# Attention and a multiplicative feed-forward network: score matmuls on (64,32) array tiles, a new order of the opening loads, and the g vectors spread by a matmul

## The chip, the core and the metric

The kernel runs on one core of one Trainium2 chip. The metric is the device time of one execution in microseconds (us), the median of ten executions. In the profile, PE is the matrix engine and PEld its weight loads, DVE the vector engine, ACT the scalar engine, POOL the GpSimd engine, and SP an engine that here only issues DMAs. The engines run side by side, each works through its own instructions in order, and semaphores tie them together.

## The reference

Attention over 8 batches of 12 heads with 448 rows of 64 elements, where q and k are normalised (RMS norm) first; then a feed-forward network over the 3584 rows of 768:

```python
def _attn_ref(q, k, v, g_q, g_k):
    def rmsnorm(x, g):
        rms = np.sqrt(np.mean(x * x, axis=-1, keepdims=True) + 1e-06)
        return x / rms * g
    q_n, k_n = (rmsnorm(q, g_q), rmsnorm(k, g_k))
    scores = 1.0 / np.sqrt(q.shape[-1]) * np.matmul(q_n, k_n.transpose(0, 1, 3, 2))
    scores = scores - np.max(scores, axis=-1, keepdims=True)
    attn = np.exp(scores)
    attn = attn / (np.sum(attn, axis=-1, keepdims=True) + 1e-09)
    return np.matmul(attn, v).astype(np.float32)

def _moe_ref(x, w1, w2, w3, w_out):
    a = x @ w1
    b = x @ w2
    h = a * b @ w3
    return (h @ w_out).astype(np.float32)
```

q, k and v are (8, 12, 448, 64), w1 and w2 are (768, 1024), w3 is (1024, 1024), w_out is (1024, 768). All inputs and the output are float32.

## The kernel before

**Quads.** The attention is cut into 24 quads, each of four heads of one batch (three quads a batch). A row index of a head is split over 112 partitions and J = 4 column groups. For each quad the kernel loads q and k on SP's queue (`load_qk`, L98, three buffers each) and v on POOL's queue with a cast to bf16 (`load_v`, L116, four buffers); squares q and k on ACT (L157); sums them on DVE (L166); forms alpha = 1/rms on ACT as exp(-0.5 ln) (L176, L177); scales q by alpha (L188), by the product of both g vectors `g_b` (L195), and k by alpha (L201). The result `qks` is transposed to `qkT` (two heads stacked on 128 partitions): on PE for quads 0 to 4 (L220, copied out by DVE at L223), by a DMA transpose on SP's queue (L210) for the later ones.

**Slots.** The main loop goes over 25 x 4 slots, t = 4i + sl. A slot writes its work in this order: the scores and exp of a quarter of quad i (`qk_exp`, L226); up to one of the three products of quad i-1 (`pv_set`, L248: the row sums, then the two halves of P times v); up to four of the waiting weight loads (`wq`); filler work for PE; and last the preparation steps that the table `agenda` puts into this slot. Each engine executes in the order of this text, so that an instruction that waits holds up all that is written behind it on its engine.

**The scores.** One slot makes two `sc` tiles of 112 x 2 x 512 in PSUM (two buffers). Each comes from two matmuls at L235: 64 contraction rows (one head each, partitions 0 to 63 and 64 to 127), 112 output columns, 448 streamed columns. ACT takes exp of each tile (L244). The other large matmuls are in column tiles of 32: `pv` at L259 (112 x 32), and all of the feed-forward network in `narrow` (L312, L314: 128 x 32, four tiles side by side, one set for each 128-row block).

**The product of w3 and w_out.** The kernel makes w34 = w3 @ w_out once, in the opening slots: eight transposes of w3 (`w3_transpose`, L290, PE at L293, copied out by DVE at L288) and sixteen units (`w34_unit(fc, nh)`, L298, PE at L301, copied out by ACT at L286). nh is the half of w_out's columns that a unit uses. `W34_SLOTS` gives one or two of these 24 steps to each of slots 1 to 13; the list `w34q` orders them, with units of half 1 coming `LAG` steps behind those of half 0. From slot 15 on the fillers are the feed-forward network of the batches whose attention is done (`ffn1_a`, `ffn1_b`, `ffn2`); what is left of it runs after the last quad, from about 348 us.

**The opening.** POOL first loads both g vectors, each spread over 112 partitions by its DMA (L401, L402). DVE multiplies them at L424 and makes `g_b` at L425, written ahead of the first L188. q of quad 0 goes on SP's queue and k on ACT's, in two halves each; SP then issues q and k of quads 1 and 2 (the loads of quad 2 are written in slot 0). POOL then copies one column of the last head of k (L410, the tile `gate`), which holds POOL's queue until that half of k has landed. Behind it stand: the first half of w_out (two DMAs), w3 blocks 0 to 3, v of quad 0, the second half of w_out (two DMAs); and in the slots w3 blocks 4 and 5, v of quad 1, w3 blocks 6 and 7, v of quad 2, sixteen DMAs of w1 and w2, v of quad 3. POOL's loads share eight semaphores, so that each issue waits until the one eight places before it has landed. Sixteen warm-up matmuls (L395) keep PE busy meanwhile.

Of the kernel before, what the change touches and what calls it, by code (L numbers as in the profile page):

```python
# [8 lines left out]
FP = mybir.dt.float32  # L9
BF = mybir.dt.bfloat16  # L10
MULT = mybir.AluOpType.mult
# [7 lines left out]
def kernel(  # L19
# [13 lines left out]
    nc = tc.nc  # L33

    B, H, S, D = q.shape
    NP = 112
    J = S // NP
    HQ = 4
# [4 lines left out]
    CF = DFF // 128  # L43
# [4 lines left out]
    const = ctx.enter_context(tc.tile_pool(name="const", bufs=1))  # L48
# [12 lines left out]
    N_PE_T = 5  # L61
    N_SQ_ACT = 24
    W34_EV = "DA"
    LAG = 4
    SHIFT = [0, 0, 0, -1, -2, -3, -4]
    PREP_1 = {
        "sq0": -4, "red0": -4, "sq1": -4, "red1": -3, "alpha": -3,
# [11 lines left out]
    w_outs = const.tile([128, CF, DM], BF, name="w_outs")  # L79
    w3s = big_pool.tile([128, CF, DFF], BF, tag="big", name="w3s")  # L80
    w3T = big_pool.tile([128, CF, DFF], BF, tag="big", name="w3T")
    gq_b = const.tile([NP, D], FP, name="gq_b")
    gk_b = const.tile([NP, D], FP, name="gk_b")
    g_b = const.tile([NP, D], BF, name="g_b")
    ident = const.tile([128, 128], BF, name="ident")
    ones = const.tile([NP, HALF], BF, name="ones")
# [1 line left out]
    gate = const.tile([NP, 1], FP, name="gate")  # L88
# [9 lines left out]
    def load_qk(i, split=1, k_eng=None):  # L98
        b, m = divmod(i, NQB)
        s = st[i]  # L100
        s["q"] = load_pool.tile([NP, HQ, J, D], FP, tag="q", name="q_sb")
        s["k"] = load_pool.tile([NP, HQ, J, D], FP, tag="k", name="k_sb")
        n = HQ // split
        for h0 in range(0, HQ, n):
            for t_sb, src, eng in (
                (s["q"], q, nc.sync),
                (s["k"], k, k_eng or nc.sync),
            ):
                eng.dma_start(
                    out=t_sb[:, h0 : h0 + n].rearrange("p h j d -> p h (j d)"),  # L110
                    in_=src[b, HQ * m + h0 : HQ * m + h0 + n].rearrange(
                        "h (p j) d -> p h (j d)", j=J
                    ),
                )

    def load_v(i):  # L116
        b, m = divmod(i, NQB)
        s = st[i]
        s["v"] = load_pool.tile([NP, HQ, J, D], BF, tag="v", name="v_sb", bufs=4)
        nc.gpsimd.dma_start(  # L120
            out=s["v"].rearrange("p h j d -> p h (j d)"),
            in_=v[b, HQ * m : HQ * (m + 1)].rearrange("h (p j) d -> p h (j d)", j=J),
        )
# [9 lines left out]
    def load_w3(c):  # L133
        nc.gpsimd.dma_start(
            out=w3s[:, c, :],
            in_=moe_w3.rearrange("(c p) f -> p c f", p=128)[:, c, :],
        )

    def load_wout(nh, c):
        nc.gpsimd.dma_start(  # L140
            out=w_outs[:, 4 * c : 4 * c + 4, nh * NH : (nh + 1) * NH],
            in_=moe_w_out.rearrange("(c p) n -> p c n", p=128)[
                :, 4 * c : 4 * c + 4, nh * NH : (nh + 1) * NH
            ],
        )


    def prep_sq(i, pr, on_act=False):
# [77 lines left out]
    def qk_exp(i, g):  # L226
        s = st[i]
        if g == 0:
            s["P"] = att_pool.tile([NP, HQ, J, S], BF, tag="P", name="P")
        pr, t = divmod(g, 2)  # L230
        qkT, P = s["qkT"], s["P"]
        for jk in (2 * t, 2 * t + 1):
            sc = sc_psum.tile([NP, 2, 512], FP, tag="sc", name="sc")
            for u in range(2):
                nc.tensor.matmul(  # L235
                    out=sc[:, u, 0:S],
                    lhsT=qkT[u * D : (u + 1) * D, pr, J + jk, :],
                    rhs=qkT[u * D : (u + 1) * D, pr, 0:J, :].rearrange(
                        "d j p -> d (j p)"
                    ),  # L240
                    start=True,
                    stop=True,
                )
            nc.scalar.activation(  # L244
                out=P[:, 2 * pr : 2 * pr + 2, jk, :], in_=sc[:, :, 0:S], func=AF.Exp
            )
# [151 lines left out]

    with tc.manual_schedule():

        nc.gpsimd.dma_start(out=gq_b, in_=g_q.unsqueeze(0).broadcast_to([NP, D]))  # L401
        nc.gpsimd.dma_start(out=gk_b, in_=g_k.unsqueeze(0).broadcast_to([NP, D]))  # L402
        nc.vector.memset(warm_t, 0.0)
        nc.vector.memset(eps_t, 64e-6)
        nc.vector.memset(ones, 1.0)
        load_qk(0, split=2, k_eng=nc.scalar)
        nc.scalar.preload_act_table_set("natural_log_exp_and_others")
        load_qk(1)
        make_identity(nc, ident)
        nc.gpsimd.tensor_copy(out=gate, in_=st[0]["k"][:, HQ - 1, 0, 0:1])  # L410
        load_wout(0, 0)
        load_wout(0, 1)
        for c in range(4):
            load_w3(c)
        load_v(0)
        load_wout(1, 0)
        load_wout(1, 1)
        warm(16)
        for pr in range(2):
            prep_sq(0, pr, on_act=True)  # L420
            prep_red(0, pr)
            prep_alpha(0, 2 * pr, 2 * pr + 2)
            if pr == 0:
                nc.vector.tensor_tensor(out=gq_b, in0=gq_b, in1=gk_b, op=MULT)  # L424
                nc.vector.tensor_scalar(  # L425
                    out=g_b, in0=gq_b, scalar1=8.0, scalar2=None, op0=MULT
                )
            prep_scale(0, pr, pe=True)
            if pr == 0:
                prep_pe_transpose(0, 0)  # L430

        wq = [lambda c=c: load_w3(c) for c in range(4, CF)]
        wq.insert(2, lambda: load_v(1))
        wq.append(lambda: load_v(2))
        for h in range(HQ):
            for half in range(2):
                for w, src in ((w1s, moe_w1), (w2s, moe_w2)):
                    wq.append(
                        lambda w=w, src=src, h=h, half=half: load_w12(w, src, h, half)
                    )  # L440
        wq.append(lambda: load_v(3))

        w34q = [lambda: w3_transpose(0), lambda: w3_transpose(1)]
        for fc in range(CF + LAG):
            if fc < CF:
                w34q.append(lambda fc=fc: w34_unit(fc, 0))
            if fc + 2 < CF:
                w34q.append(lambda fc=fc: w3_transpose(fc + 2))
            if fc >= LAG:
                w34q.append(lambda fc=fc: w34_unit(fc - LAG, 1))  # L450

        def prep_part(n, part):
            pe = n < N_PE_T
            if part[:2] == "sq":
                prep_sq(n, int(part[2]), on_act=n < N_SQ_ACT)
            elif part[:3] == "red":
                prep_red(n, int(part[3]))
            elif part == "alpha":
                prep_alpha(n)
            elif part[:2] == "sc":  # L460
                prep_scale(n, int(part[2]), pe=pe)
            elif pe:
                prep_pe_transpose(n, int(part[1]))


        agenda = {}
        for n in range(1, NQ):
            shift = SHIFT[min(n, len(SHIFT)) - 1]
            table = PREP_1 if n == 1 else PREP
            for part, rel in table.items():  # L470
                agenda.setdefault(max(0, 4 * n + rel + shift), []).append((n, part))

        for i in range(NQ + 1):
            for sl in range(4):
                t = 4 * i + sl
                mine = agenda.pop(t, [])
                for n, part in mine:
                    if part == "load":
                        load_qk(n)
                if i < NQ:  # L480
                    qk_exp(i, sl)
                if t == 0:
                    prep_pe_transpose(0, 1)
                seen = len(fillers)
                if i > 0 and sl < 3:
                    pv_set(i - 1, sl)
                fresh = fillers[seen:]
                if sl == 0 and 4 <= i + 1 < NQ:
                    load_v(i + 1)
                for _ in range(4):  # L490
                    if wq:
                        wq.pop(0)()
                if t in W34_SLOTS:
                    for _ in range(W34_SLOTS[t]):
                        if w34q:
                            w34q.pop(0)()
                elif not w34q:
                    left = (14 - t) % 12 + 1
                    old = len(fillers) - sum(1 for f in fillers if f in fresh)
                    fill(min(2, -(-old // left)))  # L500
                for n, part in mine:
                    if part[0] == "t":
                        prep_part(n, part)
                for n, part in mine:
                    if part[0] != "t" and part != "load":
                        prep_part(n, part)
        fill(len(fillers))
# [28 lines left out]
```

## Time and profile before

| what | value |
|---|---|
| median of ten executions | 391.9 us (391.3 to 394.57) |
| the profiled execution's own time | 391.85 us |
| its span from the first to the last instruction | 390.0 us |
| the 16 warm-up matmuls L395 | end at 7.76 us |
| first scores (slot 0) start | 13.64 us |
| first transpose of w3 starts | 20.73 us |
| first feed-forward matmul starts | 68.83 us |
| last slot with scores (t = 95) | about 346 us |
| score matmuls L235 | 384, 57.4 us busy |
| exp L244 | 192 of 915 ns, 165.3 us busy |

The span begins with the first instruction and ends with the last; what lies around it is 1.85 us in this execution. "Busy" is the time in which at least one instruction of the group was under way: four matmuls side by side count once.

### The profile page before, as it was taken

What the parts mean: (1) busy time and instruction counts of PE and PEld (TensorE: products, weight loads), DVE (VectorE), ACT (ScalarE), POOL (GpSimd) and SP (SyncE); (2) the same over time, 40 slices, a digit from 0 to 9 for tenths busy, and PEclk for the clock granted to TensorE, in tenths of its full rate; (3) what the DMA queues carried; (4) which work ended last, traced back from release to release, by engine and by line L of the source; (5) the groups of instructions that cost most, each with busy time, mean ns of one, the idle gap of its engine ahead of it and who ended that gap; (6) DMA issues with size and microseconds to landing.
All of it is one profiled execution on the core that took longest, in us unless ns stands there. A gap on an engine that the chain in (4) does not pass through costs nothing.

```text
span 390.0 us, 14802 instructions
## 1 busy us (share of the span) xinstructions
PE 373.6 (96%) x6688; PEld 193.5 (50%) x6688; DVE 242.2 (62%) x383; ACT 285.0 (73%) x467; POOL 35.4 (9%) x61
## 2 busy tenths in 40 slices
PE   6489999999999999999999999999999999999995
PEld 2154554544544455445544554445445555456563
DVE  1766766887767577567766766757776672234232
ACT  4459889998888885897898768888889857751210
POOL 5232441000000000000000000000000000000000
PEclk9579999999999999999999999999999999999999
DMA  8999999476986489675878489559965651003014
GB/s 180 227 236 237 207 213 211 76 141 137 211 197 89 116 167 216 121 162 90 192 175 157 79 222 207 72 109 197 197 101 122 119 142 26 3 11 114 2 25 142
DMA packets 78367, 55.08 MB, mean 141 GB/s; under 512 B 37824, under 2 KB 72160, under 8 KB 78304
## 3 DMA queue, kind: packets, MB, share of 16 engines
q1 hardware_dynamic: 61568, 41.30, 45.5%
q0 software_dynamic: 16256, 12.38, 22.4%
q8 instruction: 52, 0.85, 0.9%
q10 hardware_dynamic: 480, 0.46, 0.4%
q14 instruction: 11, 0.09, 0.1%
HBM read 46.72 MB, written 11.01 MB: 148 GB/s over the span
## 4 chain that ended last, share of the span: by engine, by line
PE 88%; DMA 5%; ACT 3%; DVE 2%; POOL 0%; issue 0%; ACTq 0%
PE pa L314 19%; PE po L314 19%; PE pb L314 19%; PE pv L259 15%; PE sc L235 12%; PE wps L301 4%; DMA w3s<-in_moe_w_dram 3%; DMA k_sb<-in_k_dram 1%; PE w3T_ps L293 1%; ACT P L244 1%; ACT sq L157 1%; ACT w34s L286 1%; PE qkT_ps L220 1%; DVE qtmp L188 1%; DVE qks L201 0%; POOL w_outs L140 0%
## 5 line engine op out<-in xcount | busy, mean ns | idle before, releaser
L244 ACT ACTIVATE P<-sc 112x896 bf16<-112x896 f32 x192 | 165.3, 915 | 42.3 <-PE sc L235 42.3
L344 DVE TENSOR_TENSOR abT<-pb,a_sb 128x448 bf16<-128x448 f32 x64 | 39.9, 624 | 77.1 <-PE pb L314 56.7
L314 PE MATMUL pa<-xT,w1s 128*32 128x448 bf16 x1536 | 84.0, 353 | 0.0
L314 PE MATMUL pb<-xT,w2s 128*32 128x448 bf16 x1536 | 83.8, 352 | 0.0
L314 PE MATMUL po<-w34s,abT 128*32 128x384 bf16 x1792 | 77.9, 326 | 0.0
L166 DVE TENSOR_REDUCE ssq<-sq 112x16 f32<-112x1024 f32 x48 | 58.3, 1215 | 14.1 <-ACT sq L157 14.1
L314 PEld LDWEIGHTS <-abT 128*32 128x32 bf16 x1792 | 47.4, 97 | 27.6 <-issue 2.4
L235 PE MATMUL sc<-qkT 64*112 64x448 bf16 x384 | 57.4, 378 | 0.7 <-DVE qkT L223 0.7
L314 PEld LDWEIGHTS <-w2s 128*32 128x32 bf16 x1536 | 41.2, 97 | 31.4
L314 PEld LDWEIGHTS <-w1s 128*32 128x32 bf16 x1536 | 39.8, 96 | 34.0 <-issue 4.7
L331 ACT CAST a_sb<-pa 128x448 bf16<-128x448 f32 x64 | 33.9, 530 | 26.5 <-PE pa L314 26.5
L363 DVE COPY o_sb<-po 128x384 f32<-128x384 f32 x56 | 31.2, 556 | 31.5 <-PE po L314 31.5
L259 PE MATMUL pv<-P,v_sb 112*32 112x448 bf16 x768 | 45.1, 355 | 0.0
L120 POOL DMA_DIRECT2D v_sb<-in_v_dram x24 | 17.0, 708 | 236.6 <-PE pv L259 215.6
L188 DVE TENSOR_TENSOR qtmp<-q_sb,alpha 112x512 bf16<-112x512 f32 x48 | 32.7, 682 | 6.0 <-ACT alpha L177 6.0
L235 PEld LDWEIGHTS <-qkT 64*112 64x112 bf16 x384 | 17.4, 126 | 31.8 <-issue 29.4
L201 DVE TENSOR_TENSOR qks<-k_sb,alpha 112x512 bf16<-112x512 f32 x48 | 32.8, 683 | 0.0
L157 ACT ACTIVATE sq<-q_sb 112x512 f32<-112x512 f32 x48 | 30.5, 635 | 1.8 <-DMA q_sb<-in_q_dram 1.8
L275 DVE TENSOR_TENSOR xT<-pv,r 128x448 bf16<-128x448 f32 x48 | 29.6, 617 | 3.2 <-PE pv L259 3.2
L157 ACT ACTIVATE sq<-k_sb 112x512 f32<-112x512 f32 x48 | 30.0, 625 | 0.0
L259 PEld LDWEIGHTS <-v_sb 112*32 112x32 bf16 x768 | 16.2, 95 | 23.7 <-issue 15.2
L301 PE MATMUL wps<-w_outs,w3T 128*128 128x384 bf16 x128 | 23.2, 330 | 0.0
(36 smaller groups left out, 175.7 us busy)
## 6 DMA issues: line engine op xcount, KB each, us to landing
q_sb<-in_q_dram SPq DMA_DIRECT2D x23, 448.0 KB, 5.7
k_sb<-in_k_dram SPq DMA_DIRECT2D x23, 448.0 KB, 6.1
v_sb<-in_v_dram POOLq DMA_DIRECT2D x24, 224.0 KB, 4.8
out_dram<-o_sb SPq DMA_DIRECT2D x8, 336.0 KB, 3.7
out_dram<-o_sb SPq DMA_DIRECT2D x8, 288.0 KB, 3.1
w3s<-in_moe_w_dram POOLq DMA_DIRECT2D x8, 256.0 KB, 15.0
out_dram<-o_sb SPq DMA_DIRECT2D x8, 240.0 KB, 4.3
w_outs<-in_moe_w_out_dram POOLq DMA_DIRECT2D x4, 384.0 KB, 13.4
```

The lines of the kernel that those rows point to most:

```text
L157: nc.scalar.activation(out=sq[:, t], in_=src[:, hs], func=AF.Square)
L166: nc.vector.tensor_reduce(out=s["ssq"][:, :, hs, :], in_=s.pop(("sq", pr)), axis=AX, op=ADD)
L188: nc.vector.tensor_tensor(out=qtmp.transpose([0, 2, 1, 3]), in0=s["q"][:, hs], in1=alpha[:, 0, hs].unsqueeze(3).broadcast_to([NP, 2, J, D] ...
L201: nc.vector.tensor_tensor(out=qks[:, 1].transpose([0, 2, 1, 3]), in0=s["k"][:, hs], in1=alpha[:, 1, hs].unsqueeze(3).broadcast_to([NP, 2, ...
L235: nc.tensor.matmul(out=sc[:, u, 0:S], lhsT=qkT[u * D : (u + 1) * D, pr, J + jk, :], rhs=qkT[u * D : (u + 1) * D, pr, 0:J, :].rearrange("d ...
L244: nc.scalar.activation(out=P[:, 2 * pr : 2 * pr + 2, jk, :], in_=sc[:, :, 0:S], func=AF.Exp)
L259: nc.tensor.matmul(out=ps[h * HALF : (h + 1) * HALF, :], lhsT=w, rhs=P[:, h, jk, :], start=(jk == 0), stop=(jk == J - 1), tile_position=(0 ...
L301: nc.tensor.matmul(out=ps[:, 0:NH], lhsT=w3T[:, gc, fc * 128 : (fc + 1) * 128], rhs=w_outs[:, gc, nh * NH : (nh + 1) * NH], start=(gc == 0 ...
L314: nc.tensor.matmul(out=ps[32 * h : 32 * h + 32, 0:n], lhsT=lhsT[:, 32 * h : 32 * h + 32], rhs=rhs, start=start, stop=stop, tile_position=( ...
L331: nc.scalar.copy(out=a_sb, in_=ps[:, 0:S])
L344: nc.vector.tensor_tensor(out=abT[bp][:, fi, odd * S : (odd + 1) * S], in0=ps[:, 0:S], in1=a_tiles.pop((b, fi)), op=MULT,)
L363: nc.vector.tensor_copy(out=o_sb[:, nh * NH : (nh + 1) * NH], in_=ps[:, 0:NH])
```

## The change

Five edits:

1. Each score matmul of 64 x 112 becomes four of 64 x 32 (the last one 64 x 16), with an explicit tile position. The two heads and four column groups make eight tiles; a slot has 16 matmuls in place of 4.
2. The two broadcasting loads of g on POOL's queue become two loads of one row of 64 elements each, on ACT's queue behind k of quad 0. DVE multiplies the rows with the factor 8, PE spreads the product over 112 partitions with a matmul against a row of ones, and DVE copies it to `g_b`.
3. POOL's gate waits for the first half of q of quad 0, no longer for the second half of k.
4. POOL's loads are reordered: the first half of w_out, w3 blocks 0, 1, 2, v of quad 0, w3 blocks 3, 4; then in the slots w3 block 5, v of quad 1, w3 blocks 6, 7, the second half of w_out, v of quad 2, and the rest as before.
5. `LAG` goes from 4 to 8: all units of w34 that use the second half of w_out come behind all that use the first half.

The number of quads that are transposed on PE (`N_PE_T` = 5) is the same in both kernels, and with `QK1_AT` = -1 the loads of quad 1 stand where they stood.

```diff
-    LAG = 4
+    LAG = 8
+    LOADS_0 = ["o0", "w0", "w1", "w2", "v0", "w3", "w4"]
+    LOADS_1 = ["w5", "v1", "w6", "w7", "o1", "v2"]
+    GATE = ("q", 0)
+    QK1_AT = -1
...
-    gq_b = const.tile([NP, D], FP, name="gq_b")
-    gk_b = const.tile([NP, D], FP, name="gk_b")
+    g_row = const.tile([1, 2, D], FP, name="g_row")
+    gp_row = const.tile([1, D], BF, name="gp_row")
+    ones_row = const.tile([1, NP], BF, name="ones_row")
...
+    def load_any(x):
+        kind, a = x[0], int(x[1])
+        if kind == "o":
+            load_wout(a, 0)
+            load_wout(a, 1)
+        elif kind == "w":
+            load_w3(a)
+        else:
+            load_v(a)
...
             for u in range(2):
-                nc.tensor.matmul(
-                    out=sc[:, u, 0:S],
-                    lhsT=qkT[u * D : (u + 1) * D, pr, J + jk, :],
-                    rhs=qkT[u * D : (u + 1) * D, pr, 0:J, :].rearrange(
-                        "d j p -> d (j p)"
-                    ),
-                    start=True,
-                    stop=True,
-                )
+                for c0 in range(0, NP, 32):
+                    c1 = min(c0 + 32, NP)
+                    nc.tensor.matmul(
+                        out=sc[c0:c1, u, 0:S],
+                        lhsT=qkT[u * D : (u + 1) * D, pr, J + jk, c0:c1],
+                        rhs=qkT[u * D : (u + 1) * D, pr, 0:J, :].rearrange(
+                            "d j p -> d (j p)"
+                        ),
+                        start=True,
+                        stop=True,
+                        tile_position=(u * D, c0),
+                    )
...
-        nc.gpsimd.dma_start(out=gq_b, in_=g_q.unsqueeze(0).broadcast_to([NP, D]))
-        nc.gpsimd.dma_start(out=gk_b, in_=g_k.unsqueeze(0).broadcast_to([NP, D]))
...
+        nc.vector.memset(ones_row, 1.0)
         load_qk(0, split=2, k_eng=nc.scalar)
+        nc.scalar.dma_start(out=g_row[:, 0], in_=g_q.unsqueeze(0))
+        nc.scalar.dma_start(out=g_row[:, 1], in_=g_k.unsqueeze(0))
         nc.scalar.preload_act_table_set("natural_log_exp_and_others")
-        load_qk(1)
+        if QK1_AT < 0:
+            load_qk(1)
         make_identity(nc, ident)
-        nc.gpsimd.tensor_copy(out=gate, in_=st[0]["k"][:, HQ - 1, 0, 0:1])
-        load_wout(0, 0)
-        load_wout(0, 1)
-        for c in range(4):
-            load_w3(c)
-        load_v(0)
-        load_wout(1, 0)
-        load_wout(1, 1)
+        if GATE is not None:
+            nc.gpsimd.tensor_copy(out=gate, in_=st[0][GATE[0]][:, GATE[1], 0, 0:1])
+        for x in LOADS_0:
+            load_any(x)
...
             if pr == 0:
-                nc.vector.tensor_tensor(out=gq_b, in0=gq_b, in1=gk_b, op=MULT)
-                nc.vector.tensor_scalar(
-                    out=g_b, in0=gq_b, scalar1=8.0, scalar2=None, op0=MULT
-                )
+                nc.vector.scalar_tensor_tensor(
+                    out=gp_row, in0=g_row[:, 0], scalar=8.0, in1=g_row[:, 1],
+                    op0=MULT, op1=MULT,
+                )
+                g_ps = mm_psum.tile([NP, D], FP, tag="mm", name="g_ps")
+                nc.tensor.matmul(
+                    out=g_ps, lhsT=ones_row, rhs=gp_row, start=True, stop=True
+                )
+                nc.vector.tensor_copy(out=g_b, in_=g_ps)
...
-        wq = [lambda c=c: load_w3(c) for c in range(4, CF)]
-        wq.insert(2, lambda: load_v(1))
-        wq.append(lambda: load_v(2))
+        wq = [lambda x=x: load_any(x) for x in LOADS_1]
...
+                if t == QK1_AT:
+                    load_qk(1)
```

## The prediction

> **What bounds the kernel now.** I read the page's shares and slices first.
>
> ```profile
> PE 373.6 (96%) x6688; PEld 193.5 (50%) x6688; DVE 242.2 (62%) x383; ACT 285.0 (73%) x467; POOL 35.4 (9%) x61
> ...
> PE   6489999999999999999999999999999999999995
> ...
> ACT  4459889998888885897898768888889857751210
> PEclk9579999999999999999999999999999999999999
> DMA  8999999476986489675878489559965651003014
> ```
>
> PE is full from the fourth slice (9.75 us each) to the end. Only the first three hold idle PE time, and there the DMA engines are full. So there are two kinds of gain: less PE time in a slot, and an earlier start of the full stretch. Next the chain of waits up to 72 us.
>
> ```profile
> 1.20 5.27 DMA k_sb<-in_k_dram
> ...
> 6.52 0.18 POOL gate L410
> 6.70 1.48 POOL w_outs L140 x2
> 8.18 12.51 DMA w3s<-in_moe_w_dram
> ...
> 20.73 1.05 PE w3T_ps L293 x8
> ...
> 22.41 1.22 DVE ssq L166
> ...
> 33.40 1.06 ACT sq L157 x2
> 34.45 0.61 PE w3T_ps L293 x8
> 35.07 1.30 PE wps L301 x8
> 36.37 0.52 PE sc L235 x4
> 36.88 0.87 PE pv L259 x16
> ```
>
> The opening is one chain: k of quad 0, the gate, POOL's issues, w3 block 0 landing at 20.68, its transpose, DVE's copy, and behind that copy the sums (L166) of quad 1. It then runs over DVE and ACT until 34.45, over PE alone until 57.9, over ACT and DVE until 68.4, and from there only PE. The step at 34.45 is named ACT, but the timeline shows the weight load beside it waiting for a DMA, w3 block 4, whose semaphore was complete at 34.40. PE's work before that ended at 33.86, so this DMA costs 0.59.
>
> ```profile
> 10.21 0.23 DVE L424 TENSOR_TENSOR gq_b<-gq_b,gk_b 112x64 f32<-112x64 f32 x1 [3.04 <-DMA gk_b<-in_g_k_dram]
> ...
> 17.59 0.74 POOL L140 DMA_DIRECT2D w_outs<-in_moe_w_out_dram  x1 [5.78 <-DMA w_outs<-in_moe_w_out_dram]
> ...
> 34.44 0.45 PEld L293 LDWEIGHTS <-w3s 128*128 128x128 bf16 x8 [1.02 <-DMA w3s<-in_moe_w_dram]
> ```
>
> DVE waits for gk until 10.21, though alpha is ready at 7.76. POOL's tenth load waits at 17.59 for a semaphore. Last, one slot of the full stretch:
>
> ```profile
> 202.15 0.18 PEld L235 LDWEIGHTS <-qkT 64*112 64x112 bf16 x4 [0.37 <-issue]
> 202.15 0.59 PE L235 MATMUL sc<-qkT 64*112 64x448 bf16 x4
> ...
> 202.66 0.50 PEld L259 LDWEIGHTS <-v_sb 112*32 112x32 bf16 x16 [0.34 <-issue]
> ```
>
> By the starts of single matmuls, the last set of pb begins at 201.858, the two score sets at 202.150 and 202.383, pv at 202.664. Sets of four follow each other every 189 ns elsewhere (448 columns), so a set's own time is 187. The slot of scores thus costs 202.664 - 201.858 - 0.187 = 0.62 us: 374 ns of streaming, 105 going in, 46 between the sets, 95 coming out.
>
> [...] 128 x 32 to 64 x 112 costs 105, back 95; a change of rows alone (w34's 128 x 128 matmuls to 64-row scores) costs 96, a change of columns alone (pv to wps) 108; pv to pa, both in 32-column tiles, costs 2. [...] No row here shows eight 64 x 32 tiles; the two halves of rows do run together now (starts 3 ns apart), and so do four columns. [...] w_outs, issued by 7.43, moves its first bytes only at 12.10, when k of quad 1 lands (12.22).
>
> **Scores (edit 1).** The mode is still another one than that of its neighbours, and a change of rows alone cost 96, so I expect both drains to stay. What can go is the 46 between the sets. It is weight load that the first set couldn't hide: 126 ns of load show 46, and in pv behind a drain 92 ns of load show 12. With 32-column loads I take 12. Against this, eight loads and eight matmuls are sent where there were four of both; at 1.7 ns each (the starts in pv) the last of a set begins 27 ns behind the first, 23 more than now, and the drain out waits for it. Sum: 105 + 187 + 12 + 187 + 95 + 23 = 609 against 621, 12 ns less. 88 slots lie where PE is the chain (6 to 12 and 15 to 95): 88 x 12 = 1.1 us less. Bounds: no later last tile gives 34 x 88 = 3.0 less; a stagger twice as long gives 0.9 more. ACT is no cover that fails: exp follows the first set's end, which moves by under 30 ns, and ACT is busy 34.1 of 40 us between 160 and 200.
>
> **g (edit 2).** It removes two POOL loads (0.69 and 0.56 issue), L424 and L425 (0.23, 0.19), and from the DMA engines 32 packets of 460 ns, 0.92 us of each engine. It adds two issues on ACT before the table load, 0.45 each as its two k issues; ACT then waits 1.75 for q, which covers 0.9. It adds one small DVE product, one matmul behind the warm-up ones and one copy. The rows land behind k's second half (6.46): 6.6 at best, 8.5 if they wait a turn behind q of quad 1. With 0.7 for product, matmul, copy and their hand-overs (by L425's 0.19 twice and 0.3 for a small matmul) g_b is there at 7.8 to 9.2 (DVE's alpha wait ends at 7.76), instead of 10.66. Slots 0 and 1 thus run some 2 us sooner. That alone brings nothing: PE then waits for w3 block 0, where it already waits 2.1 us now. It keeps slots 0 and 1 out of the way of an earlier w3.
>
> **Gate and order (edits 3 to 5).** The gate opens with q's first half at 4.74 instead of 6.46; POOL's issues start at about 4.9 instead of 6.63. Ahead of w3 block 0 stand the same two DMAs. By turns, w_outs may start when q of quad 1 is through, about 8.5 without g, instead of 12.1, and then shares with k and q of quads 1 and 2. By conserved work it is less: the engines are full, so only what they lose now can be won: 0.92 of g's packets, and at 8 to 10 us a share of 0.82, 0.4 lost. That is 1.3; by turns (w3 at about 18.5) it would be 2.2. I take 1.7: block 0 at 19.0. Nothing else is late before it: q and k of quad 1 land at 10.3 and 12.2, and even 2 us later they precede their squares (16.81 now, 14.5 then).
>
> After that a POOL load lands each 1.7 us. Now block 4 stands behind the second half of w_out (30.29, 32.65). In the new order it is eighth and needs no free semaphore: it lands two places behind where block 3 is, 25.98 + 2.66 (v) + 1.7 = 30.3, less the 1.7 gained, for a use at 33. The 0.59 goes. What is late next is ACT and PE, both nearly full there; I take 0.5. Blocks 5 to 7 come four or more us sooner too. The second half of w_out lands at about 41.5 less 1.7 and is first used in slot 9, now 47.5: 5 us of slack, which an earlier start of 2.2 leaves intact. The steps per slot stay the same with `LAG` 8: slots 7 and 8 still have one transpose and one unit. w1 and w2 keep their place behind v of quad 2; the last lands at 63.95 for a use at 68.83, slack 4.9 against 2.2 needed.
>
> **Sum.** 1.7 + 0.5 + 1.1 = 3.3 us off the span of 390.0: 386.7. With 1.85 around it this is 388.55 for a run like the profiled one (391.85), which stands at the median 391.9. Forecast 388.5. Its own range: least 1.3 + 0 - 0.9 = 0.4 off, most 2.2 + 0.6 + 3.0 = 5.8 and a faster clock in the opening (0.5 now from 10.59 to 24.25; w3's first transpose takes 1.05 instead of 0.62): 385.7 to 391.5.
>
> **Rivals.**
> - *No drain.* If 64 x 32 counts as a neighbour of 128 x 32, a slot costs 374 + 12 + some 16, about 0.40, and 88 x 0.22 = 19 us go: 391.9 - 2.2 - 19 = 371. ACT's free 15% would allow it (0.54 of a slot of 3.66). For it speaks only that pv and pa mix freely; against it the 96 for a change of rows alone.
> - *The eight tiles don't stream together* (slower). If the two halves of rows run in turn once the columns are split, each set takes 187 more, 374 a slot; with 96 slots 36 us: 391.9 - 2.2 + 36 = 426. A part of this suffices: from 2.2 / 92 = 24 ns a slot on, the opening's gain is spent; 50 ns more a slot ends at 394.3. For it: no row shows this form, and instructions for the same work go from 4 to 16. Against it: four columns and two row halves each run together today.
> - *The opening is masked.* w3 block 0 comes no sooner, since q and k of quads 1 and 2 and the same w_out are ahead of it [...]; the scores win their 1.1 or nothing: 391. For it: the DMA share of 1.1 to 1.3 from 10 to 20 us.
>
> **Chances.** The forecast 0.66; no drain 0.10; tiles not together 0.14; masked 0.10. The range takes the forecast's own and the near part of the rivals: 384 to 394.5. A measurement of this kernel tells about 0.3%, 1.2 us, from no change. Faster: 0.10 + most of the forecast, 0.70. Same: the masked case and the forecast's weak end, 0.15. Slower: 0.15.
>
> **What would show it.** w3's first transpose near 19.0 and L188 at about 8.5 confirm the opening; still 20.7 is the masked case. No wait of L293 for w3 near 33, and the feed-forward's first matmul at about 66.5 instead of 68.83, confirm the order. In a slot of the full stretch the scores should take about 0.61 with waits of 0.3 to 0.4 of weight loads at both sides; 0.40 with none is no drain, 0.65 or more is the slower rival. Wrong would be also a wait of wps for the second half of w_out in slot 9, or a wait of L188 for g.

## The result

| | before | after |
|---|---|---|
| median | 392.11 us (52 runs) | 388.36 us (15 runs, 387.21 to 391.25) |
| ratio | | 0.9905, 95% interval 0.9887 to 0.9923 |
| profiled execution | 391.85 us, span 390.0 | 388.85 us, span 387.1 |

The forecast was 388.5. The sum is right, but in part by luck: one of its terms was half of what was measured, and a loss that it didn't have took most of the difference back. The page of the kernel after, shares and slices (the columns are those of the page before; line numbers are up to 18 higher, so L314 is now L332, L235 is L252 and L293 is L311):

```profile
PE 372.8 (96%) x7841; PEld 189.9 (49%) x7841; DVE 242.7 (63%) x384; ACT 285.0 (74%) x467; POOL 34.1 (9%) x59
...
PE   6599999999999998999999999999999999999994
...
q8 instruction: 61, 1.00, 1.1%
```

PE is full one slice earlier than before, and one later slice, the sixteenth, has a hole (8). Queue 8 moves instructions in blocks of 16,384 bytes: 61 of them, before 52. That they are PE's is read from their number, which follows PE's instructions (15,682 matmuls and weight loads, before 13,376): nine blocks more for 2306 instructions more, 256 a block.

The chain of waits of the kernel after, first 72 us:

```profile
0.74 3.52 DMA q_sb<-in_q_dram
...
4.31 0.18 POOL gate L431
4.50 1.55 POOL w_outs L145 x2
6.04 11.34 DMA w3s<-in_moe_w_dram
...
17.43 1.04 PE w3T_ps L311 x8
...
33.27 0.38 PE sc L252 x4
33.64 0.87 PE pv L277 x16
34.51 0.55 PE w3T_ps L311 x8
35.07 1.30 PE wps L319 x8
```

It is the same chain, begun 2.2 us earlier at the gate and 3.3 us earlier at the first transpose of w3. The fifth transpose no longer stands in it after a wait (it is at 30.89). One slot of the full stretch, in the timeline:

```profile
199.58 0.14 PEld L252 LDWEIGHTS <-qkT 64*32 64x32 bf16 x16 [0.37 <-issue]
199.58 0.57 PE L252 MATMUL sc<-qkT 64*32 64x448 bf16 x16
...
200.08 0.50 PEld L277 LDWEIGHTS <-v_sb 112*32 112x32 bf16 x16 [0.36 <-issue]
```

There are sixteen weight loads and matmuls in the time of four, and the idle time of the weight loads on both sides (0.37, 0.36) is still there. From the starts of single matmuls: 105 ns going in, 13 between the two sets, 112 coming out, 604 ns a slot in place of 621.

How far the kernel after runs ahead of the kernel before, by the starts of the same matmuls in both traces:

| at | first w3 transpose | slot 3 | slot 5 | slot 6 | slot 13 | first feed-forward | slot 32 | slot 40 | slot 95 | end of span |
|---|---|---|---|---|---|---|---|---|---|---|
| us ahead | 3.30 | 2.83 | 2.89 | 3.56 | 3.38 | 3.40 | 3.67 | 2.34 | 3.25 | 2.87 |

So the opening brings 3.4, and from there the lead grows by 17 ns a slot (0.27 over the 16 slots from 16 to 32), as the shorter score slots say. But between slots 32 and 40 it loses 1.46 at once, and 0.4 more behind the last matmul, in the last stores. The 1.46 is one pause, in the timeline of the weight loads:

```profile
144.91 1.26 PEld L332 LDWEIGHTS <-abT 128*32 128x32 bf16 x29
147.70 0.28 PEld L332 LDWEIGHTS <-abT 128*32 128x32 bf16 x11 [1.52 <-issue]
```

In the middle of an output block, with all operands there, PE issues nothing from 146.1 to 147.7. "issue" means that the profile shows no semaphore that it waited for.

### The profile page after: what moved, and what is told of

Same layout as the page of the kernel before. It is cut to its first block, busy times and chain, and to the rows that moved or that the text cites. A ratio compares the mean times of both kernels' runs of the same rounds, so it can differ in the third digit from the quotient of the medians.

```text
span 387.1 us, 17111 instructions
## 1 busy us (share of the span) xinstructions
PE 372.8 (96%) x7841; PEld 189.9 (49%) x7841; DVE 242.7 (63%) x384; ACT 285.0 (74%) x467; POOL 34.1 (9%) x59
## 4 chain that ended last, share of the span: by engine, by line
PE 89%; DMA 4%; ACT 3%; DVE 1%; issue 0%; POOL 0%
PE pa L332 19%; PE po L332 19%; PE pb L332 19%; PE pv L277 15%; PE sc L252 12%; PE wps L319 4%; DMA w3s<-in_moe_w_dram 3%; ACT P L262 1%; PE w3T_ps L311 1%; DMA q_sb<-in_q_dram 1%; ACT sq L172 1%; PE qkT_ps L235 1%; ACT w34s L304 1%; POOL w_outs L145 0%; DVE qtmp L203 0%
## 5 line engine op out<-in xcount | busy, mean ns | idle before, releaser
L332 PE MATMUL pa<-xT,w1s 128*32 128x448 bf16 x1536 | 84.0, 353 | 0.0
L332 PE MATMUL pb<-xT,w2s 128*32 128x448 bf16 x1536 | 83.7, 352 | 0.0
L332 PE MATMUL po<-w34s,abT 128*32 128x384 bf16 x1792 | 78.1, 326 | 1.3 <-issue 1.3
L332 PEld LDWEIGHTS <-abT 128*32 128x32 bf16 x1792 | 47.5, 97 | 29.1 <-issue 4.1
L252 PE MATMUL sc<-qkT 64*32 64x448 bf16 (+1 forms) x1536 | 55.9, 360 | 0.9 <-DVE qkT L238 0.7
L332 PEld LDWEIGHTS <-w1s 128*32 128x32 bf16 x1536 | 39.7, 96 | 34.4 <-issue 5.0
L332 PEld LDWEIGHTS <-w2s 128*32 128x32 bf16 x1536 | 41.2, 97 | 31.4
L293 DVE TENSOR_TENSOR xT<-pv,r 128x448 bf16<-128x448 f32 x48 | 29.6, 616 | 3.2 <-PE pv L277 3.2
L252 PEld LDWEIGHTS <-qkT 64*32 64x32 bf16 (+1 forms) x1536 | 13.2, 87 | 32.6 <-issue 30.6
L319 PE MATMUL wps<-w_outs,w3T 128*128 128x384 bf16 x128 | 24.1, 339 | 0.0
```

The costliest lines, as they stand in the source:

```text
L252: nc.tensor.matmul(out=sc[c0:c1, u, 0:S], lhsT=qkT[u * D : (u + 1) * D, pr, J + jk, c0:c1], rhs=qkT[u * D : (u + 1) * D, pr, 0:J, :].rearr ...
L319: nc.tensor.matmul(out=ps[:, 0:NH], lhsT=w3T[:, gc, fc * 128 : (fc + 1) * 128], rhs=w_outs[:, gc, nh * NH : (nh + 1) * NH], start=(gc == 0 ...
L332: nc.tensor.matmul(out=ps[32 * h : 32 * h + 32, 0:n], lhsT=lhsT[:, 32 * h : 32 * h + 32], rhs=rhs, start=start, stop=stop, tile_position=( ...
```

## The experiments

Theory A: the opening brings all of the gain that is kept; the scores win 16 ns a slot with both drains (the gaps of 105 and 95 ns before and after the score sets) still there, and give it back in pauses for want of instructions (theory P). The rivals are: the scores bring the gain (C); the pause belongs to the transfers of that stretch and not to the number of instructions (Q); w_outs waits its turn on the DMA engines, as the prediction had it (T), against a fixed delay from its issue (L). All results are in one table; "first" and "fifth" are the starts of these w3 transposes, FF that of the first feed-forward matmul, pauses what PE loses at one place after the first FF, where it is over 0.1 us (from the starts of its matmuls, against the kernel before), ratios against the kernel before run beside it.

| run | edits | first | fifth | FF | pauses | median | ratio (95%) |
|---|---|---|---|---|---|---|---|
| before | | 20.73 | 34.45 | 68.83 | none | 392.11 | |
| after | 1 to 5 | 17.43 | 30.89 | 65.43 | 1.46 | 388.36 | 0.9905 (0.9887, 0.9923) |
| e1 | 1 | 20.30 | 34.24 | 68.91 | 0.73, 0.39 | 391.61 | 0.9997 (0.9980, 1.0014) |
| e2 | 2 to 5 | 17.71 | 30.78 | 65.37 | none | 388.99 | 0.9905 (0.9887, 0.9922) |
| e4 | 2 | 18.10 | 33.14 | 67.52 | none | 390.69 | 0.9952 (0.9935, 0.9969) |
| e5 | 3 | 19.75 | 33.87 | 68.26 | none | 391.89 | 0.9997 (0.9977, 1.0018) |
| e6 | 4, 5 | 19.79 | 32.86 | 67.45 | none | 390.59 | 0.9954 (0.9942, 0.9966) |
| e7 | 2, 3 | 17.24 | 32.41 | 68.30 | none | 391.05 | 0.9969 (0.9953, 0.9985) |
| e3 | 1 with 64 columns, 2 to 5 | 17.08 | 30.11 | 64.61 | none | 387.21 | 0.9866 (0.9845, 0.9888) |
| e8 | as e3, no gate | 15.98 | 29.50 | 64.05 | none | 386.24 | 0.9854 (0.9821, 0.9887) |
| e0 | after again | 17.76 | 30.79 | 65.29 | 0.15, 0.58, 1.00, 0.94 | 389.06 | 0.9905 (0.9870, 0.9940) |
| e9 | as e3, in halves | 17.86 | 30.91 | 65.45 | 0.27, 0.68, 1.20 | 389.74 | 0.9931 (0.9909, 0.9953) |
| e10 | e3 again | 17.75 | 31.27 | 65.82 | none | 387.81 | 0.9885 (0.9857, 0.9914) |

### Scores and opening apart (e1, e2)

e1 is the kernel before with the diff's part in `qk_exp`; e2 is the kernel after with

```diff
-                for c0 in range(0, NP, 32):
-                    c1 = min(c0 + 32, NP)
-                    nc.tensor.matmul(
-                        out=sc[c0:c1, u, 0:S],
-                        lhsT=qkT[u * D : (u + 1) * D, pr, J + jk, c0:c1],
...
+                nc.tensor.matmul(
+                    out=sc[:, u, 0:S],
+                    lhsT=qkT[u * D : (u + 1) * D, pr, J + jk, :],
```

> The kernel before with edit 1 alone. Theory A (the scores win about 16 ns a slot, and both drains stay): the first w3 transpose stays at 20.7, the slot of scores takes 605 ns instead of 621, with about 105 in, 13 between and 112 out; the time is 1.4 us lower, 390.7, except where PE runs out of instructions, which may cost 1 to 1.5 us in an execution. Theory B (edit 1 nets nothing or loses, and the whole gain of the change is the opening's): 391.9 to 393.5. Theory C (the scores bring most of the gain): 389 to 390.

> The kernel after with the scores as they were before (edits 2 to 5 alone). Theory A: the first w3 transpose near 17.4, slots 15 to 95 all run 3.3 us earlier than before with no drift along the way, no PE pause of over 1 us, and the time is 388.6 (3.3 below before), about the same as the kernel after. Theory C: 390 to 391.

e1's time is that of before within its interval (0.7 us to either side); e2 has the ratio of the whole change. Theory C falls: edit 1 nets nothing here that the times can show. In e1's trace the slots are 604 ns (105, 13, 112), and yet from slot 15 to slot 95 it needs 277.38 us where before needs 277.59: 0.21 less where 80 x 17 ns = 1.36 were due. Two pauses, of 0.73 (at 149.7) and 0.39 (at 156.0), are 1.12 of the 1.15 that are missing. e2 has no pause and no drift: its lead is 3.46 from slot 15 to slot 95.

### What holds PE up (e3, e0, e9, e10)

e3 takes 64 columns a tile, e9 the same tiles with each matmul cut into two of 224 streamed columns, which makes 16 matmuls a slot again:

```diff
-                for c0 in range(0, NP, 32):
-                    c1 = min(c0 + 32, NP)
+                for c0 in range(0, NP, 64):
+                    c1 = min(c0 + 64, NP)
```
```diff
-            for u in range(2):
-                for c0 in range(0, NP, 64):
+            for hh in range(2):
+                h0, h1 = hh * (S // 2), (hh + 1) * (S // 2)
+                for u in range(2):
+                    for c0 in range(0, NP, 64):
...
-                        out=sc[c0:c1, u, 0:S],
+                            out=sc[c0:c1, u, h0:h1],
...
-                        rhs=qkT[u * D : (u + 1) * D, pr, 0:J, :].rearrange(
+                            rhs=qkT[u * D : (u + 1) * D, pr, 2 * hh : 2 * hh + 2, :].rearrange(
```

> The kernel after with score tiles of 64 (and 48) columns in place of 32: eight matmuls a slot, not sixteen. Theory A: [...] both stay (105 in, some 98 out), between the sets some 20 to 30 ns of weight load show: 605 to 615 ns a slot, no worse than 32 columns by more than 10 ns; PE's instructions fall by 1536, its fetches from 61 to about 55, so a pause for instructions is rarer: median 387.3 to 388. Rival (the pause has nothing to do with the number of instructions): the same spread as the kernel after, 388.4.

> The kernel after, unchanged, for a second profile. Theory P (PE runs out of fetched instructions now and then, because 32-column tiles add 2304 of them): another pause of PE of 0.3 to 1.5 us within a feed-forward stretch, at another place than 146 us[...]. Rival Q (the pause at 146 us belongs to the loads and stores issued there): it is at 146 us again, or in none of the other places. Time 388.4.

> Score tiles of 64 columns as in the run with them, but each matmul cut into two of 224 streamed columns: as many instructions as with 32 columns in the kernel after (16 matmuls a slot), another tiling. Theory P: pauses of PE come back, 0.3 to 1.5 us in the profile, the fetches are 61, and the time is 0.5 to 1.5 us above the run with whole 64-column tiles. Rival R (the narrow tiles themselves cause the pauses): no pause, and the time differs from that run only by what the slot takes longer (up to 60 ns a slot, seen inside the slot).

> The kernel after with score tiles of 64 columns, unchanged from the earlier run, as the comparison for the two beside it: no pause of PE over 0.15 us, 55 fetches, 387.2, 1 us below the kernel after.

e3's slot in the timeline:

```profile
197.29 0.14 PEld L252 LDWEIGHTS <-qkT 64*64 64x64 bf16 x8 [0.37 <-issue]
197.30 0.57 PE L252 MATMUL sc<-qkT 64*64 64x448 bf16 x8
...
197.79 0.50 PEld L277 LDWEIGHTS <-v_sb 112*32 112x32 bf16 x16 [0.36 <-issue]
```

105 in, 23 between, 102 out, 604 ns: the wider tiles, whose weight loads take 105 and 98 ns against 89 and 82, show 10 ns more between the sets and come out 10 sooner, since the last of four matmuls starts 10 ns behind the first and the last of eight 20. In the slot, then, the tile's width is worth nothing. From slot 15 to slot 95 e3 and e10 need 276.25 us each, 1.34 less than before: without pauses nearly all of the 1.36 arrives. The timelines of the weight loads of e0 and of e9:

```profile
145.57 1.26 PEld L332 LDWEIGHTS <-abT 128*32 128x32 bf16 x29
147.90 1.25 PEld L332 LDWEIGHTS <-abT 128*32 128x32 bf16 x35 [1.07 <-issue]
...
152.85 0.49 PEld L277 LDWEIGHTS <-ones 112*32 112x32 bf16 x13 [0.36 <-issue]
154.37 0.10 PEld L277 LDWEIGHTS <-ones 112*32 112x32 bf16 x3 [1.03 <-issue]
```

```profile
145.51 1.07 PEld L334 LDWEIGHTS <-abT 128*32 128x32 bf16 x25
147.34 1.25 PEld L334 LDWEIGHTS <-abT 128*32 128x32 bf16 x35 [0.75 <-issue]
...
152.30 0.49 PEld L279 LDWEIGHTS <-ones 112*32 112x32 bf16 x13 [0.17 <-issue]
154.08 0.10 PEld L279 LDWEIGHTS <-ones 112*32 112x32 bf16 x3 [1.29 <-issue]
```

e9 has other tiles than the kernel after, as many instructions, and the same kind of pauses (sum 2.1 us, e0 2.7); e3 and e10 have neither. Rival R, the narrow tile itself, falls.

The count of PE's instructions says where PE stops. Number them as the trace records them (matmuls, weight loads and a few others). All ten pauses of the four profiles begin after number 3265, 3521, 4289, 5057 or 5313. Each of these is 193 more than a multiple of 256, and a block holds 256 instructions by the counts of both kernels, so PE stops every time at the same place of a block, which is read here as its edge. In e1, which lacks the matmul and the weight load for g, the pause at 5057 comes one matmul later in the program than in the other three, as the count asks. And every pause ends 1.3 to 1.5 us after a block of queue 8 has landed. In the kernel after it began at 146.09; a block that began to move at 145.1, 9.9 us after the one before it, landed at 146.2, and PE went on 1.5 us later. In the nine profiles with 52 or 55 blocks every block landed 1.5 us or more before PE came to its edge, and there is no pause. From these places and landings it is read that PE waits for its instructions: theory P. e0 was expected to pause at another place than 146; three of its four pauses do, but one is there again, at edge 5057. That is the same place of the same program, and doesn't speak for Q.

Rival Q keeps a part. In all four profiles the pauses over 0.5 us lie between 130 and 156 us, most near 147 and 153. In the kernel after the DMA share is 0.94 and 0.95 there:

```profile
142.00:148.00 6.00, 4.72 (x116) 2.56 (x112) 3.48 (x7) 2.21 (x5) 0.70 (x1) 1.00 0.94 233
148.00:154.00 6.00, 6.00 (x147) 2.96 (x138) 4.39 (x7) 4.27 (x7) 0.00 (x0) 1.00 0.95 177
```

(stretches of the kernel after: length, busy us and instructions of PE, PEld, DVE, ACT and POOL, granted clock, DMA share, GB/s). Before has a share of 0.90 and 0.89 there and no pause, and from 148 to 154 e2 and e10 have 1.27 and 1.23 and none either. In all profiles a block begins to move at the earliest some 285 instructions before its edge. Ahead of the ten pauses it began 4.1 to 5.9 us later than that. In e3 a block was 4.0 us late in the same way (at 151.0) and still landed 2.4 us before its edge, because PE took longer to get there. So both seem to be needed: more instructions a microsecond, and something that holds a block up. That this something is the other transfers is argued; no run changed them alone. The expected time of e9 (0.5 to 1.5 above e10) was missed: 389.74 against 387.81, 1.9 more. Times alone don't separate e10 from e0 (their intervals overlap), nor were e3's 387.2 met again by e10 (387.81); the pauses in the traces do.

### The opening, edit by edit (e4, e5, e6, e7)

e4 is edit 2 alone and e5 edit 3 alone; e6 is the diff's order of loads and `LAG` 8 in the kernel before; e7 is e2 with

```diff
-    LAG = 8
-    LOADS_0 = ["o0", "w0", "w1", "w2", "v0", "w3", "w4"]
-    LOADS_1 = ["w5", "v1", "w6", "w7", "o1", "v2"]
+    LAG = 4
+    LOADS_0 = ["o0", "w0", "w1", "w2", "w3", "v0", "o1"]
+    LOADS_1 = ["w4", "w5", "v1", "w6", "w7", "v2"]
```

> The kernel before with edit 2 alone (g as rows, spread by a matmul; the gate stays on k's second half). Theory G (the two broadcast loads held POOL's queue on the DMA engines back, so w_outs began late): first w3 transpose at 18.5 to 19.2, with the gate still at about 6.2, and the time 1.5 to 2 us lower. Rival H (the gate's 2 us brought the earlier w3): first w3 transpose at 20.2 to 20.7, L188 at 8.3 all the same, and the time within 0.5 us of before.

> The kernel before with edit 3 alone (gate on q's first half; g still by two broadcast loads). The first bytes of w_outs came 4.67 us after the end of POOL's second... first issue in both kernels (7.43 to 12.10, 5.31 to 9.98). Theory L (a fixed delay from the issue): first w_outs bytes about 2 us earlier than 12.1, near 10. Theory T (it waits its turn behind q and k on the DMA engines, as the prediction had it): still about 12. Under both, since the slow packets of g stay and the DMA engines have the same work, the first w3 transpose comes only 0.4 to 1 us sooner (19.7 to 20.3), and the time is 391 to 391.6.

> The kernel before with edits 4 and 5 alone (order of POOL's loads and LAG). Prediction's step: the first w3 transpose stays at 20.4 to 20.7; the fifth (34.45 now) no longer waits for w3 block 4 and starts 0.5 to 0.7 us sooner; the first feed-forward matmul 0.4 to 0.6 sooner, the time 391.5. Rival: the gain at the fifth transpose is taken back by ACT within two slots and the first feed-forward matmul moves by less than 0.2.

> Edits 2 and 3 without 4, 5 and 1 (the opening's old order of loads and LAG 4, scores of full width). If the order matters once w3 block 0 is early: the fifth w3 transpose waits for its block and starts near 32 instead of 30.8, and the first feed-forward matmul is at 66.0 to 66.8 instead of 65.4: 389.5 to 390.2. If the order brings nothing: 388.9, as edits 2 to 5 together.

**g.** Edit 2 alone brings the first transpose 2.6 us forward (to 18.10; 18.5 to 19.2 was expected), with the gate where it was (6.53) and the first bytes of w_outs too (12.10). The stretches of before and of e4:

```profile
6.00:8.00 2.00, 1.76 (x6) 0.44 (x4) 1.17 (x1) 0.77 (x3) 1.48 (x3) 1.00 1.09 220
8.00:10.00 2.00, 0.00 (x0) 0.00 (x0) 0.00 (x0) 0.80 (x2) 2.00 (x5) 1.00 0.82 210
```

```profile
6.00:8.00 2.00, 0.82 (x5) 0.27 (x3) 1.09 (x2) 1.05 (x4) 1.47 (x3) 1.00 1.12 267
8.00:10.00 2.00, 0.50 (x5) 0.21 (x4) 1.80 (x4) 0.51 (x1) 2.00 (x5) 1.00 1.12 266
```

220 and 210 GB/s become 267 and 266. The 32 packets that spread g took 0.83 us each on average, the sixteen of gk between 6.6 and 9 us 0.6 to 1.45; that they slowed q and k around them is read from these rates. The last of q and k of quads 1 and 2 lands at 13.4 instead of 16.7, and w_outs then has the engines for itself. g itself is ready sooner, though it still holds DVE for a moment, here in the kernel after (10.21 and 10.58 before):

```profile
7.65 0.21 DVE L440 SCALAR_TENSOR_TENSOR gp_row<-g_row 1x64 bf16<-1x64 f32 x1 [0.97 <-DMA g_row<-in_g_k_dram]
...
8.28 0.68 DVE L203 TENSOR_TENSOR qtmp<-q_sb,alpha 112x512 bf16<-112x512 f32 x1
```

**The gate.** Edit 3 alone moves the first bytes of w_outs from 12.10 to 9.71. Theory L holds: in all thirteen profiles they come 4.15 to 4.91 us after the end of POOL's first w_outs issue, whether that ends at 2.33 (e8) or at 7.53 (e4). The first transpose comes 1.0 sooner, the time not by more than its interval (0.8 us): the fifth waits 1.43 for its block instead of 1.02. Edit 3 was tried by itself only in the old order of loads.

**The order.** The fifth transpose, in e7 and then in e2 (weight loads of w3, blocks 3 to 5):

```profile
27.24 0.45 PEld L308 LDWEIGHTS <-w3s 128*128 128x128 bf16 x8 [0.37 <-issue]
32.41 0.45 PEld L308 LDWEIGHTS <-w3s 128*128 128x128 bf16 x8 [2.30 <-DMA w3s<-in_moe_w_dram]
37.28 0.45 PEld L308 LDWEIGHTS <-w3s 128*128 128x128 bf16 x8 [0.37 <-issue]
```

```profile
27.54 0.45 PEld L308 LDWEIGHTS <-w3s 128*128 128x128 bf16 x8 [0.37 <-issue]
30.78 0.45 PEld L308 LDWEIGHTS <-w3s 128*128 128x128 bf16 x8 [0.37 <-issue]
34.30 0.45 PEld L308 LDWEIGHTS <-w3s 128*128 128x128 bf16 x8 [0.37 <-issue]
```

In the old order, w3 block 4 still lands behind the half of w_out that nobody needs yet. Of the 3.5 us that edits 2 and 3 gain at the first transpose, e7 keeps 0.5 at the first feed-forward matmul: PE waits 2.3, and the next transpose is another 1.35 us further behind than in e2 (4.87 after the fifth, 3.52 there), with PE's granted clock at 0.5 from 32.9 to 36.3. This second stretch at half clock seems not to be usual for e7: its profiled execution has a mean clock of 0.976, and 19 of its 22 executions have 0.979 or more. By the ratios e7 gains 1.2 us and e2 3.7, with intervals apart, so the order is worth some 2.5 us there rather than the 3 of the profiles. With the new order all of it arrives: e2 is 3.0 ahead at the first transpose and 3.5 at the first feed-forward matmul. e6 shows the order alone: 1.4 at the first feed-forward matmul, of which 0.94 is at the first transpose already; nothing ahead of that block differs from before, and e1, where the opening is unchanged, moved it by 0.43. e3 and e10, one and the same kernel, have 17.08 and 17.75. So the first transpose scatters by some half a microsecond or more between executions, and no single one of these times is good to better than that. e6's median, 390.59, is clearly below before, so more than the 0.6 at the fifth transpose is in it. A small part of it may be that 19 of the 59 executions of before beside it have a mean clock under 0.979 and take 393.2 us on average, the other 40 take 392.1, and of e6's 22 only one has such a clock; what the rest is stays open. The times expected of e5 (391 to 391.6), e6 (391.5) and e7 (389.5 to 390.2) were missed: the gate alone brought less and the new order more than was thought, and the old order cost more.

### No gate (e8)

```diff
-    GATE = ("q", 0)
+    GATE = None
```

> The kernel after with score tiles of 64 columns and without the gate: POOL issues w_outs at about 1.3. If the engines move more when POOL's and SP's loads are mixed (355 GB/s of source bytes against 265 of SP's alone, between 6 and 10 us), the first w3 transpose comes 0.5 to 0.8 us sooner, at 16.3 to 16.6, and the time is 386.6. If the loads of quad 0 suffer, the first squares (4.28) and L188 (8.5) come 0.5 to 1 us later; that stays hidden, as PE waits for w3 anyway, unless it is over 2 us: then the time is 387.5 or more.

e8 adds this to e3. w_outs' first bytes come at 6.48, L188's counterpart is at 8.18 (8.28 in the kernel after), the first transpose is at 15.98. Its median, 386.24, is the lowest of all and below both kernels; against e3 its interval overlaps, so the gate's own share isn't settled, only that quad 0 doesn't suffer without it.

## Why the prediction was right, and where it wasn't

- **"Block 0 at 19.0", 1.7 us.** The mechanism was in part another one, and the size too small: 3.30. "32 packets of 460 ns, 0.92 us of each engine" was the author's estimate; it priced g by its own packets, and these too low: in the trace of before they took 0.83 us on average. e4 shows 2.6 us, with the loads beside the packets slower as well (210 against 266 GB/s). This is the term that was mis-sized. "By turns, w_outs may start when q of quad 1 is through" was wrong: the start is 4.2 to 4.9 us from the issue in every profile. That w_outs takes turns with the other loads was the author's estimate from one trace, where its start at 12.10 met the landing of k of quad 1 (12.22); that was chance. (The load that waits at 17.59 is POOL's eleventh, not its tenth.)
- **"After that ... The 0.59 goes. ... I take 0.5."** Right: the lead grows from 2.89 to 3.56 at the fifth transpose's place, 3.3 remain. As a part of the whole it was underrated, since without it 3 of the opening's 3.5 us are lost again in e7's profile, 2.5 by the ratios of e7 and e2. The working had the block's landing as 30.3 less 1.7; its issue no longer waited and it was there in time.
- **Scores, 12 ns a slot.** Right in kind, both drains stayed (105 and 112 ns with 64 x 32 tiles, 105 and 102 with 64 x 64). The stagger cost 17 ns, not 23, so the slot won 17: 88 x 17 = 1.5 instead of 1.1.
- **What the sum left out.** The working had the number of matmuls and loads, 16 for 4, and priced only their 1.7 ns at the head of a set. That PE's instructions have to be fetched, and can come too late, was in no step: the prediction put it at nothing without a reason. It cost 1.46 in the profiled run and 1.12 in e1's, of some 1.4 that the shorter slots win; by the times of e1 and e2 it takes back all of it, to within 0.7 us. It is near to the slower rival's place (a score slot with more instructions), but not its mechanism: the eight tiles stream together (the eight matmuls of the slot's first set start within 23 ns), and the slot itself is shorter (604 ns against 621).
- **The faster clock in the opening** didn't come: 0.5 until 23.59 (before 24.25), and that took 0.5 of the 3.3 back by slot 3: the first w34 unit needs 2.77 us there, all at half clock, and 1.86 before, where the clock rises within it. In e2 the clock rises at 21.7, and slot 3 keeps all of the 3.0 of the first transpose.
- The signs named beforehand: L188's counterpart at 8.28 (8.5 was named), no wait at the fifth transpose, the first feed-forward matmul at 65.43 (66.5), the slot at 0.60 (0.61). No wait of wps for the second half of w_out appears in the chain. The other sign of being wrong, a wait of L188 for g, did appear: alpha is there at 7.28, but g's row holds DVE until 7.65, and L188's counterpart starts at 8.28. It costs nothing, since PE waits for w3 until 17.43 all the same.

Sum of the profiled run: 3.40 at the first feed-forward matmul, 1.33 from the slots after it, less 1.46 for the pause, less 0.40 in the last stores, is 2.87, against 3.3 forecast. The opening brought more than its 1.7 + 0.5, the pause was not in the sum, and that the two nearly offset each other in the medians (388.36 against 388.5) is luck.

## What to carry to other kernels

A load that is due early is worth its full gain only if the next one in the queue is early as well: order the whole queue by first use, then open it sooner (in the profiles 3.5 us at the first transpose became 0.5 at the first feed-forward matmul with one half-tensor in the way; without it 3.0 became 3.5; by the ratios the gain is 1.2 and 3.7). Weigh a small broadcast load by what it does to the loads beside it, and spread the row on an idle engine instead. And when a matmul is cut into more instructions, count them against PE's fetches: choose the widest tile that gives the same slot. Here that is 64 columns in place of 32: no pause in three profiles, and medians of 387.2 and 387.8 against 388.4 and 389.1, though their intervals touch or overlap.

## What the runs showed of the hardware

- PE can starve for instructions, as the pauses are read. Queue 8 moves blocks of 16,384 bytes as PE goes on (in the kernel after from 22.6 to 379.8 us): 61 for 15,682 matmuls and weight loads, 52 for 13,376, which makes 256 instructions a block. No block began to move sooner than some 285 instructions before its edge, little more than one block ahead. The ten pauses, of 0.15 to 1.46 us, all begin after an instruction whose number is 193 more than a multiple of 256.
- From a block's landing to PE's going on there were 1.3 to 1.5 us in all ten pauses.
- A change of the tile's rows alone, of its columns alone or of both cost PE nearly the same: 96 ns for rows (w34 to the scores) and 108 for columns (pv to w34) in the kernel before. Going into the scores it was 105 ns with any of the three tiles. Coming out it was 95, 102 and 112 ns with 2, 4 and 8 tiles side by side, of which 3, 10 and 20 are the stagger of the last set: 92 each time.
- Between the end of POOL's first w_outs issue and the first bytes there are 4.15 to 4.91 us in thirteen profiles, whatever else was under way.
- Two loads of 28 KB that spread 256 bytes over 112 partitions cost the opening 2.6 us in one pair of profiles (e4 against before), where the first transpose scatters by half a microsecond or more; their 32 packets took 0.83 us each on average.
